# A new order for the start of a retention and feed-forward kernel: the heads' keys and states ahead of and between the first up units, and another hand-written order for block 1

## The chip, the cores and the metric

The kernel runs on one core of a Trainium2 chip. The metric is the device time of one execution in microseconds. The kernel before has a median of 298.65 us in three runs (297.25 to 298.95). A profiled execution of the same program gives the trace that all readings come from; its times count from the start of its span.

## The reference

Eight batches of eight heads, a sequence of 576, a head dimension of 64. Retention attention: scores of queries and keys, weighted by a decay that falls with the distance of the positions, times the values. The result is read as 4608 tokens of width 512 and goes through a feed-forward part with 2048 hidden units.

```python
scores = scale * np.matmul(q, k.transpose(0, 1, 3, 2))
gamma = 1.0 - 2.0 ** (-5.0 - np.arange(H, dtype=np.float32))
Dmat = np.where(rel >= 0, gamma[:, None, None] ** rel[None, :, :], 0.0)
ret = scores * Dmat[None, :, :, :]
return np.matmul(ret, v).astype(np.float32)
...
h = x @ w_in
relu6 = np.clip(h + 3.0, 0.0, 6.0)
g = h * relu6 / 6.0
return (g @ w_out).astype(np.float32)
```

## The kernel before, in words

The tokens are worked on in nine blocks of 512. Block 0 holds the "heads", the first 64 tokens of all eight batches; blocks 1 to 8 hold the other 512 tokens of one batch each, in four chunks of 128 (numbered 4 to 35). Each block goes through three stages.

*Retention.* Inside a chunk the scores are computed directly; what earlier tokens contribute comes through a state of 64x64 per head, which is multiplied by a decay from chunk to chunk. For the heads: `values_heads` (L449, result hpv), `scores_heads`, `inner_heads` (result hpo, copied into xT of block 0), `keys_heads` (L457: the keys turned by four groups of eight matmuls hpk, each followed by two scalings with a column of `dec` on ScalarE, L462), and `head_states` (L272: products pu, multiplied by the chunk's decay `gpow` into `zh`). For a chunk c, with the letter that stands for each step in the written order:
- c, `casts` (L182): key cast, query and value times decay, on ScalarE, GpSimd and VectorE. For the chunks in `Q_DVE` the second half of the query is done by VectorE (L192).
- t, `transposes` (L198): keys and queries turned by TensorE into ptk and ptq, copied to kT (ScalarE) and qT (VectorE) at L211.
- a, `scores` (L244) into pa; `masked` (L263, multiplications at L267); s, `states` (L291), products into the other half of pa (from chunk 8 on chunks go in pairs, and pu has banks of its own).
- u, `add` (L314): two additions on VectorE (L317, L320) and one decay multiplication on GpSimd (L321) carry the state z to the next chunk.
- z, `past` (L323): the state copied to fp16 by ScalarE (L327; L329 and L330 for a block's first chunk).
- x, `cross_over`: queries times the past state into po; i, `inner`: scores times values into the same po, then two casts into xT of the block (L373).

*Up product.* 16 units per block. A unit (`up_steps`, L495) is eight matmuls (a head's rows at a time, L153) into a bank ph, a Relu on ScalarE (L514, u) and a combined minimum and product on VectorE (L516) that gives g and frees the bank. `up_two` (L529) does two units for only one half of the block's tokens: L is the left half, R the right half, U a whole unit. The left half needs xT of the first two chunks only. H holds back the g instructions of half units, G gives them out.

*Down product.* For blocks 0 and 1 `down_plain` (L573): 64 steps of two matmuls, into four banks pd_0 to pd_3 of 16 steps each. pd_0 and pd_1 are filled in turn, four steps each, then pd_2 and pd_3; so pd_0 ends with step 28, pd_1 with 32, pd_2 with 60, pd_3 with 64, and each is copied out by ScalarE (L585) right behind its last step. D is a step of the older block, E one of the younger. From block 2 on `down_strassen` (L591) does seven products of halves, whose operands are sums of weights (`weight_sums`, L673) and of g; these sums are made on VectorE (L556) by `+`. The end of the last block has an order of its own (L637 to L651): the adds of c21 and c22 free the banks that the last product (3, by_e) takes.

The order is written by hand. `tc.manual_schedule` covers all five engines: each engine runs its instructions in the order in which the program issues them. `go` (L721) plays a string of letters with numbers; there is one for block 1's up product beside block 0's down product, and one for block 2's beside block 1's. After that tables (STEADY) serve every block. PSUM has six banks "pp" (ph, pa, pu, po, ptk, ptq, hpk, hpo) and two banks "st" (hpv, pd and the products of `down_strassen`); an instruction that takes a bank waits for the last reader of what was in it.

The transfers: GpSimd issues the input weights win (five DMAs, L687) and the output weights wout (four, L692) early, then the 16 small instructions `arg` (L123, L124) of `decays`, then mask and `gpow`. SyncE issues the loads of chunks fk, fq, fv (L174, L178); the first of them waits for the first piece of wout (`fetch(8, wout[0])`).

Of the kernel before, what the change touches and what calls it, by code (L numbers as in the profile page):

```python
# [12 lines left out]
FP32 = mybir.dt.float32  # L13
FP16 = mybir.dt.float16
# [7 lines left out]
def kernel(  # L22
# [64 lines left out]
    zh = [const.tile([P, NP, D], FP32, name=f"zh{b}") for b in range(B)]  # L87
# [32 lines left out]
    def decays():  # L120
        for h in range(H):
            lg = float(np.log(gamma[h]))
            nc.gpsimd.tensor_scalar(arg[:, :, h], fj[:, 0:4], lg, float(np.log(D ** -0.5)), ALU.mult, ALU.add)  # L123
            nc.gpsimd.tensor_scalar(arg[:, :, H + h], fj[:, 0:4], -lg, 0.0, ALU.mult, ALU.add)  # L124
        nc.scalar.activation(dec, arg, ACTF.Exp)
# [100 lines left out]
    Q_DVE, K_POOL, KT_DVE = (4, 6), (7, 8, 9, 10, 11, 13), (12, 13)  # L226
# [45 lines left out]
    def head_states(c):  # L272
        pu = [psum.tile([P, NP, D], FP32, tag="pp", name=f"pu{e}_{c}") for e in range(2)]
        todo = ([], [])
        for i in range(NP):
            for a in range(2):
                j, h2 = divmod(i + NP * a, 2)
                for e in range(2):
                    todo[e].append(mm(pu[e][rows(a), i], kn[rows(e), j, c, h2 * D:h2 * D + D],
                                      vh[rows(e), c, j, h2, :], start=True, stop=True))  # L280
        in_turn(todo)
        nc.vector.tensor_tensor(zh[c], pu[0], decay, ALU.mult)
        if c < 2:
            nc.vector.tensor_tensor(zh[c + NCB], pu[1], decay, ALU.mult)
        else:
            nc.scalar.copy(zh[c + NCB], pu[1])
            nc.gpsimd.tensor_tensor(zh[c + NCB], zh[c + NCB], decay, ALU.mult)
# [3 lines left out]
    def states(c0):  # L291
# [14 lines left out]
        if len(g) == 1:  # L306
            masked(c0)
# [6 lines left out]
    def add(c):  # L314
        kb, i0 = divmod(c, NCB)
        z = state_of(c)
        nc.vector.tensor_tensor(z[:, 1], sums[c][0], z[:, 0] if i0 else zh[kb - 1], ALU.add)  # L317
# [4 lines left out]

    def past(c):  # L323
        kb, i0 = divmod(c, NCB)
        z16 = work.tile([P, 2, NP, D], FP16, tag="z16", bufs=2, name=f"z16_{c}")
        if i0:
            nc.scalar.copy(z16, zs[c])  # L327
        else:
            nc.scalar.copy(z16[:, 0], zh[kb - 1])  # L329
            nc.scalar.copy(z16[:, 1], zs[c][:, 1])  # L330
        z16s[c] = z16
# [125 lines left out]
    def keys_heads(i):  # L457
# [449 lines left out]
```

## Time and profile before

| | |
|---|---|
| median of three runs | 298.65 us (297.25 to 298.95) |
| profiled execution | 297.9 us |
| its span in the trace | 296.2 us, 12622 instructions |
| granted TensorE clock | 1.0 |
| TensorE matmuls | 285.1 us busy, 5574 |
| VectorE | 216.0 us busy, 374 |
| ScalarE | 186.6 us busy, 330 |
| GpSimd | 135.7 us busy, 172 |
| DMA | 47.86 MB, mean 162 GB/s |

How to read the rows below. A timeline row is: start in us from the span's start, length in us, engine, line in the kernel, operation, result <- operands, partitions and elements, xcount (instructions of one kind that stand in a row), and in brackets how long the engine was idle before and what ended that. Matmul ends are modelled and the matmuls are pipelined, so the length of a group includes the time that its last result takes; the distance from one start to the next is the better measure. PE is TensorE, DVE VectorE, ACT ScalarE, POOL GpSimd, SPq the DMA issues of SyncE. The page's row of the chain gives the shares of the span by what held the work up that ended last.

### The profile page before, as it was taken

How to read it: one execution, taken by the hardware profiler on the slowest of the kernel's cores; microseconds unless marked ns; L12 is line 12 of the kernel's file. 1: busy time of each engine (PE TensorE's matmuls, PEld its weight loads, DVE VectorE, ACT ScalarE, POOL GpSimd, SP SyncE). 2: the span in 40 equal slices, each digit the busy share in tenths (PEclk: the TensorE clock that was granted, in tenths of full speed). 3: DMA queues.
4: the chain of work that ended last, by engine and by line, in shares of the span. 5: the costliest groups of instructions: out<-in, count | busy, mean ns of one | idle time of the engine just before them, and what ended most of it. 6: DMA issues, size and time to landing. Idle time of an engine off the chain costs nothing.

```text
span 296.2 us, 12622 instructions
## 1 busy us (share of the span) xinstructions
PE 285.1 (96%) x5574; PEld 221.2 (75%) x5574; DVE 216.0 (73%) x374; ACT 186.6 (63%) x330; POOL 135.7 (46%) x172
## 2 busy tenths in 40 slices
PE   4998999999999999999999999999999999999995
PEld 2775655878665669887877878878788978778894
DVE  8738768868875778598886887697868786647654
ACT  3838855676775778575776668567756674655420
POOL 8971046795834625239624762566255003100510
PEclk9999999999999999999999999999999999999999
DMA  7999999999999999988999999699915101200114
GB/s 165 147 174 213 224 217 233 241 232 222 170 151 243 180 211 159 243 217 182 248 226 205 203 223 152 162 199 229 130 46 100 73 6 52 92 2 2 73 73 142
DMA packets 119542, 47.86 MB, mean 162 GB/s; under 512 B 92352, under 2 KB 114880, under 8 KB 119488
## 3 DMA queue, kind: packets, MB, share of 16 engines
q1 hardware_dynamic: 114336, 41.56, 70.8%
q0 software_dynamic: 4720, 5.11, 10.7%
q8 instruction: 43, 0.70, 1.0%
q10 hardware_dynamic: 432, 0.39, 0.5%
q14 instruction: 11, 0.09, 0.2%
HBM read 36.70 MB, written 9.44 MB: 156 GB/s over the span
## 4 chain that ended last, share of the span: by engine, by line
PE 78%; DMA 6%; POOL 6%; DVE 5%; ACT 2%; issue 2%; POOLq 0%; ACTq 0%; DVEq 0%
PE ph L153 38%; PE pm L153 29%; PE pd L153 4%; DMA win<-in_moe_w_in_dram 3%; DMA fq<-in_q_dram 3%; PE po L232 3%; PE pu L232 2%; DVE g L516 2%; POOL hv L443 2%; PE pa L232 1%; POOL hk L403 1%; POOL q L192 1%; DVE g L543 1%; ACT u L514 1%; DVE a L267 1%
## 5 line engine op out<-in xcount | busy, mean ns | idle before, releaser
L153 PE MATMUL ph<-xT,win 128*64 128x512 f16 (+1 forms) x1248 | 145.7, 364 | 2.0 <-DMA win<-in_moe_w_in_dram 1.7
L516 DVE SCALAR_TENSOR_TENSOR g<-u,ph 128x512 f16<-128x512 f32 x132 | 89.7, 684 | 52.7 <-ACT u L514 52.0
L514 ACT ACTIVATE u<-ph,half 128x512 f32<-128x512 f32 x132 | 90.2, 690 | 41.7 <-PE ph L153 40.8
L153 PEld LDWEIGHTS <-win 128*64 128x64 f16 x1248 | 84.6, 136 | 28.6 <-DMA win<-in_moe_w_in_dram 2.3
L153 PEld LDWEIGHTS <-g 128*64 128x64 f16 x928 | 52.5, 110 | 14.7 <-issue 0.3
L153 PEld LDWEIGHTS <-s 128*64 128x64 f16 x896 | 50.8, 110 | 8.0 <-issue 0.2
L321 POOL TENSOR_TENSOR z<-z,gpow 128x256 f32<-128x256 f32 x24 | 16.1, 670 | 67.7 <-DVE z L320 52.5
L153 PE MATMUL pm<-ws,s 128*64 128x256 f16 x672 | 45.9, 273 | 0.0
L192 POOL TENSOR_TENSOR q<-fq,dec 128x512 f16<-128x512 f32 x30 | 35.6, 1204 | 17.3 <-DMA fq<-in_q_dram 17.3
L373 ACT CAST xT<-po 128x512 f16<-128x512 f32 (+1 forms) x36 | 21.8, 680 | 23.7 <-PE po L232 23.7
L620 POOL TENSOR_TENSOR u<-u,p 128x512 f32<-128x512 f32 x7 | 8.9, 1268 | 60.3 <-ACT u L660 54.0
L195 POOL TENSOR_TENSOR v<-fv,dec 128x512 f16<-128x512 f32 x32 | 36.0, 1125 | 0.0
L153 PE MATMUL pd<-wout,g 128*64 128x512 f16 x256 | 34.1, 381 | 0.0
L153 PE MATMUL pm<-wout,g 128*64 128x256 f16 x448 | 32.2, 273 | 0.0
L267 DVE TENSOR_TENSOR a<-pa,mask 128x512 f16<-128x512 f32 (+1 forms) x36 | 21.0, 625 | 4.9 <-PE pa L232 2.6
L556 DVE TENSOR_TENSOR s<-g 128x1024 f16<-128x1024 f16 x28 | 19.4, 695 | 0.2
L327 ACT CAST z<-z 128x512 f16<-128x512 f32 x24 | 15.0, 624 | 5.8 <-DVE z L317 5.7
L188 ACT CAST k<-fk 128x512 f16<-128x512 f32 x26 | 16.2, 622 | 1.0 <-DMA fk<-in_k_dram 1.0
L153 PE MATMUL pm<-ws,g 128*64 128x256 f16 x224 | 16.7, 274 | 0.0
L153 PE MATMUL pm<-wout,s 128*64 128x256 f16 x224 | 16.5, 273 | 0.1
L556 DVE TENSOR_TENSOR s<-g,s 128x1024 f16<-128x1024 f16 x14 | 13.0, 925 | 0.0
L543 DVE SCALAR_TENSOR_TENSOR g<-u,ph 128x512 f16<-128x512 f32 x12 | 8.0, 683 | 4.7 <-ACT u L542 4.6
(112 smaller groups left out, 288.1 us busy)
## 6 DMA issues: line engine op xcount, KB each, us to landing
fk<-in_k_dram SPq DMA_DIRECT2D x32, 256.0 KB, 4.8
fq<-in_q_dram SPq DMA_DIRECT2D x16, 512.0 KB, 5.9
fv<-in_v_dram SPq DMA_DIRECT2D x32, 256.0 KB, 5.6
out_dram<-o SPq DMA_DIRECT2D x14, 512.0 KB, 4.0
wout<-in_moe_w_out_dram POOLq DMA_DIRECT2D x4, 512.0 KB, 18.0
out_dram<-o SPq DMA_DIRECT2D x7, 256.0 KB, 4.2
win<-in_moe_w_in_dram POOLq DMA_DIRECT2D x3, 512.0 KB, 11.6
hq<-in_q_dram SPq DMA_DIRECT2D x6, 128.0 KB, 4.3
```

The source lines that it names most:

```text
L153: nc.tensor.matmul(out[r], lhs[:, r], rhs, skip_group_check=True, **flags)
L188: (nc.gpsimd.tensor_copy if c in K_POOL else nc.scalar.copy)(by_head(k16), in_rows(st[c]["fk"]))
L192: (nc.vector if e and c in Q_DVE else nc.gpsimd).tensor_tensor(by_head(q16[:, e]), in_rows(st[c]["fq"][:, :, e, :]), in_rows(dd[:, 2 + e, ...
L195: nc.gpsimd.tensor_tensor(v16, st[c]["fv"], dd[:, 1, H:2 * H, :], ALU.mult)
L232: return lambda: nc.tensor.matmul(*args, skip_group_check=True, **flags)
L267: nc.vector.tensor_tensor(a16[:, a, 0:n].rearrange("p x i q -> p (x i) q"), pa[a].rearrange("p x i q -> p (x i) q"), m, ALU.mult)
L321: nc.gpsimd.tensor_tensor(new, new, decay, ALU.mult)
L327: nc.scalar.copy(z16, zs[c])
L373: nc.scalar.copy(xt[:, s], po[s].rearrange("p x n (e r) -> p x n e r", e=2))
L514: nc.scalar.activation(uu[:, 0:n], ph[:, 0:n], ACTF.Relu, bias=half, scale=1.0 / 6.0)
L516: nc.vector.scalar_tensor_tensor(out=g[:, hf, ths, jr, :], in0=by_half(uu), scalar=1.0, in1=by_half(ph), op0=ALU.min, op1=ALU.mult)
L556: nc.vector.tensor_tensor(*pend.popleft())
```

## The change

- `decays` is split. The eight `arg` columns for keys now stand on GpSimd ahead of the wout issues, the eight for queries and the mask behind them; `gpow` ahead of the last wout issue. The exponents are two instructions in place of one: for keys behind inner_heads(0)'s copy on ScalarE, for queries behind unit 12 of block 0.
- `keys_heads` moves from between block 0's down steps to the place ahead of the first up units; keys 0 and 1 take "st" banks and are scaled by ScalarE, keys 2 and 3 take "pp" banks and are scaled by VectorE.
- `head_states` now does two chunks at a time and stands behind the first four up units. Its decay multiplications are four steps of 128x512 (`heads_decayed`): two on VectorE, two as a ScalarE copy with a GpSimd multiplication, behind units 3, 4, 9 and 10. `zh` is one tile.
- Q_DVE loses chunk 6; the second half of its query goes to GpSimd.
- The masks of single chunks get a letter of their own, m, and stand behind the adds u. The two copies of `past` for a block's first chunk are split (y for the heads' state). p and r turn keys and queries apart. The weight sums are queued as 3, 1, 2, 4 per half.
- The two order strings are new. The first begins with 24 plain down steps; blocks of eight down steps stand ahead of r4, z4 and z5; the half units L come right behind i5 and i6, and R4 right behind t8; the last unit of block 1 stands at the end of the first string.
- In the last block's end, the first half of c22 is added before c21, the second behind it.

```diff
...
@@ -117,12 +117,17 @@
         for h in (2 * i, 2 * i + 1):
             nc.scalar.activation(hmask[:, h, :], dist, ACTF.Exp, bias=scale, scale=float(np.log(gamma[h])))
 
-    def decays():
+    def decays(of):
         for h in range(H):
             lg = float(np.log(gamma[h]))
-            nc.gpsimd.tensor_scalar(arg[:, :, h], fj[:, 0:4], lg, float(np.log(D ** -0.5)), ALU.mult, ALU.add)
-            nc.gpsimd.tensor_scalar(arg[:, :, H + h], fj[:, 0:4], -lg, 0.0, ALU.mult, ALU.add)
-        nc.scalar.activation(dec, arg, ACTF.Exp)
+            if of == "q":
+                nc.gpsimd.tensor_scalar(arg[:, :, h], fj[:, 0:4], lg, float(np.log(D ** -0.5)), ALU.mult, ALU.add)
+            else:
+                nc.gpsimd.tensor_scalar(arg[:, :, H + h], fj[:, 0:4], -lg, 0.0, ALU.mult, ALU.add)
+
+    def exponents(of):
+        part = slice(0, H) if of == "q" else slice(H, 2 * H)
+        nc.scalar.activation(dec[:, :, part], arg[:, :, part], ACTF.Exp)
 
     def decays_of_chunk():
         for h in range(H):
@@ -223,7 +228,7 @@
 
 
     PAIRS = 8
-    Q_DVE, K_POOL, KT_DVE = (4, 6), (7, 8, 9, 10, 11, 13), (12, 13)
+    Q_DVE, K_POOL, KT_DVE = (4,), (7, 8, 9, 10, 11, 13), (12, 13)
     group = lambda c: [c] if c < PAIRS else [c, c + 1]
     rows = lambda x: slice(SUB * x, SUB * x + SUB)
     gs = {}
@@ -269,22 +274,27 @@
 
     decay = gpow.unsqueeze(2).to_broadcast([P, NP, D])
 
-    def head_states(c):
-        pu = [psum.tile([P, NP, D], FP32, tag="pp", name=f"pu{e}_{c}") for e in range(2)]
+    def head_states(c0, tag):
+        pu = [psum.tile([P, 2, NP, D], FP32, tag=tag, name=f"pu{e}_{c0}", **(dict(bufs=2) if tag == "st" else {}))
+              for e in range(2)]
         todo = ([], [])
-        for i in range(NP):
-            for a in range(2):
-                j, h2 = divmod(i + NP * a, 2)
-                for e in range(2):
-                    todo[e].append(mm(pu[e][rows(a), i], kn[rows(e), j, c, h2 * D:h2 * D + D],
-                                      vh[rows(e), c, j, h2, :], start=True, stop=True))
+        for c in (c0, c0 + 1):
+            for i in range(NP):
+                for a in range(2):
+                    j, h2 = divmod(i + NP * a, 2)
+                    for e in range(2):
+                        todo[e].append(mm(pu[e][rows(a), c - c0, i], kn[rows(e), j, c, h2 * D:h2 * D + D],
+                                          vh[rows(e), c, j, h2, :], start=True, stop=True))
         in_turn(todo)
-        nc.vector.tensor_tensor(zh[c], pu[0], decay, ALU.mult)
-        if c < 2:
-            nc.vector.tensor_tensor(zh[c + NCB], pu[1], decay, ALU.mult)
+        return pu
+
+    def heads_decayed(c0, e, pu):
+        z, by = zh[:, c0 + NCB * e:c0 + NCB * e + 2], gpow.unsqueeze(1).unsqueeze(3).to_broadcast([P, 2, NP, D])
+        if e:
+            nc.scalar.copy(z, pu[e])
+            nc.gpsimd.tensor_tensor(z, z, by, ALU.mult)
         else:
-            nc.scalar.copy(zh[c + NCB], pu[1])
-            nc.gpsimd.tensor_tensor(zh[c + NCB], zh[c + NCB], decay, ALU.mult)
+            nc.vector.tensor_tensor(z, pu[e], by, ALU.mult)
 
     zs, z16s, sums = {}, {}, {}
 
@@ -303,8 +313,6 @@
                         todo[s].append(mm(pu[s][rows(a), x, i], k16[rows(s), i, a, :], v16[rows(s), i + NP * a, :],
                                           start=True, stop=True))
         in_turn(todo)
-        if len(g) == 1:
-            masked(c0)
 
     def state_of(c):
         if c not in zs:
@@ -314,21 +322,24 @@
     def add(c):
         kb, i0 = divmod(c, NCB)
         z = state_of(c)
-        nc.vector.tensor_tensor(z[:, 1], sums[c][0], z[:, 0] if i0 else zh[kb - 1], ALU.add)
+        nc.vector.tensor_tensor(z[:, 1], sums[c][0], z[:, 0] if i0 else zh[:, kb - 1], ALU.add)
         if i0 < NCB - 1:
             new = state_of(c + 1)[:, 0]
             nc.vector.tensor_tensor(new, sums[c][1], z[:, 1], ALU.add)
             nc.gpsimd.tensor_tensor(new, new, decay, ALU.mult)
 
+    def past_of_heads(c):
+        z16s[c] = work.tile([P, 2, NP, D], FP16, tag="z16", bufs=2, name=f"z16_{c}")
+        nc.scalar.copy(z16s[c][:, 0], zh[:, c // NCB - 1])
+
     def past(c):
-        kb, i0 = divmod(c, NCB)
-        z16 = work.tile([P, 2, NP, D], FP16, tag="z16", bufs=2, name=f"z16_{c}")
-        if i0:
-            nc.scalar.copy(z16, zs[c])
+        if c % NCB:
+            z16s[c] = work.tile([P, 2, NP, D], FP16, tag="z16", bufs=2, name=f"z16_{c}")
+            nc.scalar.copy(z16s[c], zs[c])
         else:
-            nc.scalar.copy(z16[:, 0], zh[kb - 1])
-            nc.scalar.copy(z16[:, 1], zs[c][:, 1])
-        z16s[c] = z16
+            if c not in z16s:
+                past_of_heads(c)
+            nc.scalar.copy(z16s[c][:, 1], zs[c][:, 1])
 
     xts = {}
 
@@ -454,12 +465,16 @@
                 product(pv[:, c], pick[:, j, c, :], hd[i]["v"][:, :, j, :], start=(j == 0), stop=(j == NJ - 1))
         copy(vh[:, :, i], pv)
 
-    def keys_heads(i):
-        pk = psum.tile([P, NCB, 2, D], FP32, tag="pp", name=f"hpk{i}")
+    def keys_heads(i, tag, on_dve):
+        pk = psum.tile([P, NCB, 2, D], FP32, tag=tag, name=f"hpk{i}", **(dict(bufs=2) if tag == "st" else {}))
         for c in range(NCB):
             product(pk[:, c].rearrange("p a d -> p (a d)"), hd[i]["kT"][:, c, :], ident16, start=True, stop=True)
         for a in range(2):
-            nc.scalar.mul(kn[:, i, :, a * D:a * D + D], pk[:, :, a, :], dec[:, 0, H + 2 * i + a:H + 2 * i + a + 1])
+            to, by = kn[:, i, :, a * D:a * D + D], dec[:, 0, H + 2 * i + a:H + 2 * i + a + 1]
+            if on_dve:
+                nc.vector.tensor_scalar(to, pk[:, :, a, :], by, None, ALU.mult)
+            else:
+                nc.scalar.mul(to, pk[:, :, a, :], by)
 
     def scores_heads(i):
         kT, qT = hd[i]["kT"], hd[i]["qT"]
@@ -637,11 +652,11 @@
             yield from one(7, by_c, True)
             for m in range(2):
                 add(dve, u3[:, m], by_c[m], p1[:, m])
+            yield from one(5, by_e)
+            add(dve, c22[:, 0], by_e[0], u3[:, 0])
             add(dve, c21, bd, u3)
             store(kb, 1, o2, cols=lo)
-            yield from one(5, by_e)
-            for m in range(2):
-                add(dve, c22[:, m], by_e[m], u3[:, m])
+            add(dve, c22[:, 1], by_e[1], u3[:, 1])
             store(kb, 1, o2, cols=hi)
             for m in range(2):
                 yield from one(3, by_e, True, (m,))
@@ -715,8 +730,10 @@
             if what == "+":
                 side_sums(c)
             elif c < NCH:
-                {"c": cast, "t": lambda c: transposes(c, True, "kq" if c < PE_T else "k" if c < PE_K else ""), "a": scores, "s": states, "u": add, "z": past,
-                 "x": cross_over, "i": inner, "k": keys_heads, "h": head_states, "o": lambda _: store(*kept.popleft())}[what](c)
+                {"c": cast, "t": lambda c: transposes(c, True, "kq" if c < PE_T else "k" if c < PE_K else ""),
+                 "p": lambda c: transposes(c, True, "k"), "r": lambda c: transposes(c, True, "q"),
+                 "a": scores, "s": states, "m": masked, "u": add, "y": past_of_heads, "z": past,
+                 "x": cross_over, "i": inner, "o": lambda _: store(*kept.popleft())}[what](c)
 
     def go(plan, kb=None, down=None, ahead=None):
 
@@ -781,7 +798,12 @@
         win_piece(0, 2)
         for n in (1, 2, 3):
             win_piece(n)
-        wout = [wout_piece(pc) for pc in (0, 2, 1, 3)]
+        decays("k")
+        wout = [wout_piece(pc) for pc in (0, 2, 1)]
+        decays_of_chunk()
+        wout.append(wout_piece(3))
+        decays("q")
+        mask_of_chunk()
         distances()
         idle_products(5)
         mask_of_heads(0)
@@ -812,10 +834,15 @@
         scores_heads(3)
         values_heads(1, on_act)
         inner_heads(0, on_act)
+        exponents("k")
         values_heads(2, on_dve)
         inner_heads(1, on_dve)
         values_heads(3, on_act)
         inner_heads(2, on_dve)
+        keys_heads(0, "st", False)
+        keys_heads(2, "pp", True)
+        keys_heads(3, "pp", True)
+        keys_heads(1, "st", False)
         first = [up_steps(0, u) for u in range(4)]
         for dmc in range(3):
             for unit in first:
@@ -825,23 +852,29 @@
         for unit in first:
             for _ in unit:
                 pass
-        decays()
-        mask_of_chunk()
-        decays_of_chunk()
+        heads = [head_states(0, "pp"), head_states(2, "st")]
         fetch(8, wout[0])
+        heads_decayed(0, 0, heads[0])
         for u in range(4, NFC):
             up_unit(0, u)
-        weight_sums(3)
-        weight_sums(1, 2, 4)
+            if u == 4:
+                heads_decayed(0, 1, heads[0])
+            elif u == 9:
+                heads_decayed(2, 0, heads[1])
+            elif u == 10:
+                heads_decayed(2, 1, heads[1])
+            elif u == 12:
+                exponents("q")
+        weight_sums(3, 1, 2, 4)
         down, ahead = down_plain(0), down_plain(1)
-        go("k0 D4 k1 D4 +1 k2 D4 +1 k3 D5 h0 h1 D4 c4 h2 h3 D8 t4 c5 +1 D7 a4 s4 u4 +1 D3 t5 D5 z4 x4 a5 s5 i4 u5 z5 +1 c6 +1 D7 "
-           "x5 D2 i5 D4 t6 c7 L2 H0 L2 a6 s6 u6 G0 L2 t7 z6 L2 H0 L2 x6 a7 s7 i6 u7 G0 z7 D6 L2 c8 x7 D1 i7 t8 E4 "
-           "c9 R4 t9 c10 R2 c11 E2 a8 s8 u8 E2 R2 z8 u9 t10 E4 z9 t11 c12 R2 E2 R2 c13 E4 a10 x8 s10 i8 "
-           "u10 U1 z10 t12 u11 U1 t13 z11 U1 U1 c14 E4 a12 x10 s12 i10",
+        go("D8 +2 D8 +2 D8 +1 c4 D8 p4 D8 r4 c5 y4 +1 D4 t5 a4 s4 u4 m4 D8 z4 x4 c6 a5 s5 i4 u5 m5 D8 z5 x5 D2 i5 +1 L2 p6 r6 c7 "
+           "L2 H0 L2 a6 s6 u6 m6 G0 L2 t7 z6 H0 L2 x6 a7 s7 i6 u7 m7 G0 z7 L2 c8 x7 D2 i7 +1 t8 "
+           "c9 R4 t9 c10 R2 c11 E4 a8 s8 u8 E2 R2 z8 u9 t10 E4 z9 t11 c12 R2 E2 R2 c13 E6 a10 x8 s10 i8 "
+           "u10 U1 z10 t12 u11 U1 t13 z11 U1 c14 E6 a12 x10 s12 i10 u12 c15 U1",
            1, down, ahead)
         down = ahead
-        go("u12 c15 D7 z12 +1 U1 D3 u13 U1 D3 z13 +1 U1 D2 c16 U1 D3 U1 D3 U1 D2 U1 D1 U1 D5 a14 x12 s14 i12 u14 U1 c17 z14 +1 U1 D1 u15 U1 D1 z15 o1 "
-           "U1 +1 U1 D1 U1 D1 c18 U1 U1 D5 a16 x14 s16 i14 u16 +1 D4",
+        go("D3 z12 +1 U1 D4 u13 U1 D3 z13 +1 U1 D2 c16 U1 D3 U1 D3 U1 D3 U1 D1 U1 D5 a14 x12 s14 i12 u14 U1 c17 z14 +1 U1 D1 u15 U1 z15 o1 "
+           "U1 +1 U1 D1 U1 c18 U1 U1 D7 a16 x14 s16 i14 u16 +1 D4",
            2, down)
         for kb in range(2, NB):
             for _ in down:
```

## The prediction on record

> **What bounds the kernel now.** I read the page first: the span, the busy shares, the chain by engine.
>
> ```profile
> span 296.2 us, 12622 instructions
> ...
> PE 285.1 (96%) x5574; PEld 221.2 (75%) x5574; DVE 216.0 (73%) x374; ACT 186.6 (63%) x330; POOL 135.7 (46%) x172
> ...
> PE 78%; DMA 6%; POOL 6%; DVE 5%; ACT 2%; issue 2%; POOLq 0%; ACTq 0%; DVEq 0%
> ```
>
> TensorE is the bound: 285.1 of 296.2 us, and no other engine is above 73%. The diff leaves the matrix products as they are in number and size (moved, not removed), so the time can change only where TensorE stands still: fewer or more stalls, and what is computed inside stalls that remain. I therefore read the timeline of PE gap by gap, first its front.
>
> ```profile
> 18.50 1.95 PE L153 MATMUL ph<-xT,win 128*64 128x512 f16 x16 [0.72 <-DMA win<-in_moe_w_in_dram]
> ...
> 23.42 1.95 PE L153 MATMUL ph<-xT,win 128*64 128x512 f16 x16 [0.98 <-DMA win<-in_moe_w_in_dram]
> ...
> 33.83 0.39 PE L153 MATMUL hpk<-ident,hkT 128*64 128x128 f16 x8
> 34.05 1.03 PE L153 MATMUL pd<-wout,g 128*64 128x512 f16 x8
> ...
> 38.49 0.45 PE L232 MATMUL pu<-ws,ws 64*64 64x64 f16 x32
> ...
> 39.85 0.56 PE L232 MATMUL pu<-ws,ws 64*64 64x64 f16 x32
> ```
>
> Before the first up units and again before unit 4, PE waits for the input weights: at 18.50 after 0.72 us, at 23.42 after 0.98. The keys of the heads (hpk) and their states (pu) are paid later, between down steps: one hpk group takes 34.05-33.83 = 0.22, four take 0.88; two pu groups take 0.45+0.56 = 1.0. Together 1.9.
>
> **A. The front.** The change puts hpk ahead of the first up unit and pu between units 3 and 4, into the two stalls. How much fits depends on what they wait for.
>
> ```profile
> 15.81 1.65 POOL L692 DMA_DIRECT2D wout<-in_moe_w_out_dram  x3
> ...
> 19.35 0.19 POOL L123 TENSOR_SCALAR arg<-fj 128x4 f32<-128x4 f32 x1
> ...
> 22.25 0.20 POOL L124 TENSOR_SCALAR arg<-fj 128x4 f32<-128x4 f32 x1
> ```
>
> ```profile
> 17.60 0.58 ACT L455 CAST ws<-hpv 128x512 f16<-128x512 f32 x1 [1.16 <-PE hpv L153]
> ...
> 24.12 0.27 ACT L125 ACTIVATE dec<-arg 128x64 f32<-128x64 f32 x1
> ```
>
> ```profile
> 22.55 2.48 DVE L516 SCALAR_TENSOR_TENSOR g<-u,ph 128x512 f16<-128x512 f32 x4 [4.03 <-ACT u L514]
> ```
>
> The 16 arg rows stand from 19.35 to 22.45, 0.2 each; eight of them, now ahead of the wout issues at 15.81, take 1.6 to 1.8 and end near 17.6. The exponents are behind them on ACT and, in program order, ahead of its copy of hpv3 (now 17.60): 0.27 ends at about 17.9, the copy of 0.58 at 18.5. The last hpk group takes the bank which that copy frees: 0.22, so PE turns to the up product at about 18.8 in place of 18.5. The first four units end 0.1 later (their last pieces wait for the hpo3 copy, also 0.3 later), near 22.5; the states then take about 0.85, to 23.4. Unit 4 needs a bank from the first g, which with the same shift ends at 22.55+0.69+0.3 = 23.5; so unit 4 starts near 23.6, not 23.42. Of the 1.9 all but 0.2 is therefore hidden: **-1.7 to -1.8**, I take -1.8 with the switch between tile sizes that goes. If the weights were to land sooner, the cover would be gone and all 1.9 paid here; nothing shows that.
>
> **B. Stalls of before that go.**
>
> ```profile
> 42.09 0.39 PE L153 MATMUL ptk<-ident,k 128*64 128x128 f16 x8
> 42.65 0.64 PE L153 MATMUL ptq<-ident,q 128*64 128x128 f16 x16 [0.17 <-POOL q L192]
> ...
> 47.46 0.26 PE L232 MATMUL po<-qT,z 64*64 64x64 f16 x8 [0.21 <-ACT z L330]
> ...
> 51.77 0.39 PE L153 MATMUL ptk<-ident,k 128*64 128x128 f16 x8
> 52.23 0.64 PE L153 MATMUL ptq<-ident,q 128*64 128x128 f16 x16
> ```
>
> A ptk group takes 0.22 when nothing is awaited, here it is 42.65-42.09 = 0.56 and 52.23-51.77 = 0.46 to the next: 0.34 and 0.24 are lost. x4 loses 0.21 and its switch, some 0.38 (the z copy came late: masks stood ahead of the z adds on VectorE). The new order puts eight down steps between p4 and r4, adds ahead of masks, and eight steps ahead of z4: **-0.95**.
>
> **C. New stalls in block 1.** Each is a step of PE that needs a copy made from PE's own result, with less work put between them than the copies take. The rows for the length of such a chain:
>
> ```profile
> 43.77 1.03 PE L153 MATMUL pd<-wout,g 128*64 128x512 f16 x8
> ...
> 50.88 1.05 PE L153 MATMUL pd<-wout,g 128*64 128x512 f16 x8
> ...
> 54.92 1.09 PE L153 MATMUL ph<-xT,win 128*64 128x256 f16 x16
> 55.85 0.39 PE L153 MATMUL ptk<-ident,k 128*64 128x128 f16 x8
> 56.07 1.92 PE L153 MATMUL ph<-xT,win 128*64 128x256 f16 x32
> ```
>
> ```profile
> 43.98 0.58 ACT L585 COPY o<-pd 128x512 f32<-128x512 f32 x1 [0.30 <-PE pd L153]
> ...
> 51.00 0.76 ACT L373 CAST xT<-po 128x256 f16<-128x256 f32 x2 [0.70 <-PE po L232]
> ...
> 57.16 0.63 ACT L327 CAST z<-z 128x512 f16<-128x512 f32 x1
> ```
>
> - x5: the last of the eight steps before it ends pd_2, whose copy stands ahead of the copy of z_5 on ACT. The copy begins 0.21 after PE has left the bank (43.98 against 43.77), then 0.58 less 0.1 overlap, then 0.63: **1.3**.
> - The first L2 after i5 needs xT from that very i5. The casts start 0.12 after PE has gone on (51.00 against 50.88) and take 0.76: 0.88, less 0.05 for the switch: **0.83**. Before, four down steps and t6 lay between (50.88 to 51.77 is 0.89 for the four alone).
> - The L2 after i6 needs xT from i6 at its third product: 0.88 less two products of 0.05: **0.78**. Before, six down steps lay there.
> - R4 after t8 needs xT from i7: 0.88 less t8 (0.22) and the switch: **0.6**. Before, four steps lay there.
> - x6: behind the fourth L2 come u_10, the copy of kT_7 and z_6 on ACT. In before the same three end at 57.16+0.63 = 57.79, 1.94 after their L2 ended (55.85), and t7 and two L2 (0.22+1.84) covered them. Now t7 and one L2 (0.22+0.93) do: **0.8**.
> - a6: g of the first half unit stands ahead of both qT_6 casts on VectorE; a unit (0.69 ACT, 0.69 DVE) and two casts (1.29 below) make 2.1 after r6 against two L2 of 0.9: **0.35**. a4, by the same casts behind the work for c5, **0.15**.
>
> ```profile
> 43.11 1.29 DVE L211 CAST qT<-ptq 128x512 f16<-128x512 f32 x2 [0.75 <-PE ptq L153]
> ```
>
> Sum of C: 1.3+0.83+0.78+0.6+0.8+0.35+0.15 = **+4.8**. The bounds are 1.3 (all but x5 covered by something I overlooked) and 5.6 (each chain 0.1 slower).
>
> **D. Pairs, and the end of block 1.**
>
> ```profile
> 81.16 0.22 PE L232 MATMUL pu<-v,k 64*64 64x64 f16 x2 [0.17 <-DVE g L516]
> 81.76 0.44 PE L232 MATMUL pu<-v,k 64*64 64x64 f16 x30 [0.38 <-DVE g L516]
> ```
>
> ```profile
> 82.73 1.34 ACT L373 CAST xT<-po 128x512 f16<-128x512 f32 x2 [1.26 <-PE po L232]
> 83.91 0.63 ACT L188 CAST k<-fk 128x512 f16<-128x512 f32 x1
> ...
> 85.51 0.70 ACT L514 ACTIVATE u<-ph,half 128x512 f32<-128x512 f32 x1
> ```
>
> ```profile
> 86.24 0.69 DVE L516 SCALAR_TENSOR_TENSOR g<-u,ph 128x512 f16<-128x512 f32 x1 [1.88 <-ACT u L514]
> ```
>
> The state products wait there for a bank that g frees: 0.55, and smaller waits like it come to about 1.3. Six down steps in place of four ahead of a10 and a12 take most of that away. Against it, the last unit of block 1 (U15) now follows i10: ACT has two xT casts (1.34), a key cast (0.63) and u (0.70) to do, then DVE g (0.69), 3.3 with the overlaps, before the fourth down step of the next plan can read that g; PE has two units and three steps to do meanwhile, 2.4: 0.9. s12 takes a bank behind it, no row of its own, between 0 and the 0.55 above; I take 0.5, its nearest row, and 0.2 for small ones. Net **+0.3** (between -1.1 and +0.8).
>
> **E. The end.**
>
> ```profile
> 290.85 1.94 PE L153 MATMUL pm<-wout,s 128*64 128x256 f16 x32
> ```
>
> ```profile
> 292.01 0.43 DVE L620 TENSOR_TENSOR o<-pm,u 128x256 f32<-128x256 f32 x1 [0.77 <-PE pm L153]
> ```
>
> The last block adds half of c22 before c21 and half behind it. The second half frees its bank about one add of 0.7 later than now; the second half of the last product (16 of the 32 products) waits for it about 0.2, and the two last adds and the store follow: **+0.2** (0 to 0.4).
>
> **Removed instructions elsewhere** (six 128x256 multiplications on DVE become two of 128x512, half of q_6 goes to POOL) are at nothing: both engines have idle time there, and POOL's q_6 is wanted only some 3 us after it can be ready. If that cover fails, 1.1 at most.
>
> **Sum.** -1.8 -0.95 +4.8 +0.3 +0.2 = +2.5, between -2.2 and +4.0. The profiled execution took 297.9 us (span 296.2 and 1.7 around it), the median of the runs is 298.65, 0.75 above it. On the median this gives 301.1; I say **301.0**.
>
> **The rivals.**
> 1. *Faster.* An engine that waits lets the others catch up, so after the 1.3 of x5 later copies may be ready in time. Then A, B and the waits of D remain: -1.8-0.95+1.3-0.9+0.2 = -2.2, 296.5. Against it: the chains of C begin at PE's own results (i5, i6, i7, the fourth L2), and a lead of the other engines doesn't shorten those. Chance 0.17.
> 2. *No change.* a4, a6, x6 and s12 are covered after all, the chains with nothing between (x5, two L2, R4) remain: -1.8-0.95+3.5-0.2+0.2 = +0.75, 299.4. For it: four of my waits are differences of two long sums. Chance 0.25.
> 3. *Slower still, through the loads.* The eight arg instructions hold the wout issues back by 1.7. SP's first loads go out when wout's first piece has landed:
>
> ```profile
> 30.95 0.42 SPq L174 DMA_DIRECT2D fk<-in_k_dram  x1
> ```
>
> ```profile
> 41.15 1.45 POOL L192 TENSOR_TENSOR q<-fq,dec 128x512 f16<-128x512 f32 x1 [17.29 <-DMA fq<-in_q_dram]
> ```
>
> ```profile
> wout<-in_moe_w_out_dram POOLq DMA_DIRECT2D x4, 512.0 KB, 18.0
> ```
>
> If wout lands 1.7 later, q_4 is ready at 44.3 in place of 42.6, while r4 comes near 42.9: about 1.3 more, 302.4. It decides from a delay of about 0.4 on. Against it: 18.0 us from issue to landing for 512 KB means that wout waits behind others, so a later issue should wait less. Chance 0.06. The Trainium skill ("DMA: Bandwidth & Descriptors", section "Issuing engines are not separate DMA queues") says that DMAs of all issuing engines run on the same 16 engines and interleave; by that rule the bytes ahead decide and not the moment of issue, the 18.0 agrees, and the sum would stay.
>
> **How the numbers follow.** My forecast, +2.4 give or take 1.2, has 0.52; no change 0.25; faster 0.17; slower still 0.06. The likeliest case's own range is 299.9 to 302.2. Reaching to the cases beside it until 2 in 10 are out gives 297.2 to 302.8. A measurement of this kernel can tell about 0.5% (1.5 us) from no change: faster 0.17, same 0.25, slower 0.58 from the cases above.
>
> **What would show it.** In the changed profile: the hpk rows before the first ph row, unit 4 at about 23.6, the first pd row near 34.0 with no pu behind it (A); no wait at x4 (B); po at x5 behind the z copy, ph rows with waits on ACT xT after i5, i6, i7 (C); pd behind a DVE g at the start of block 2 (D). I am wrong if PE's waits between 45 and 70 us come to less than 2 us, or if fq lands later than 41.

## The result, and the profile after

The changed kernel takes 301.32 us (median of four runs, 300.63 to 302.28) against 298.36 of before; the ratio is 1.0106, with a 95% interval of 1.0063 to 1.0149. In a second set of six runs beside later experiments the ratio was 1.0136 (1.0090 to 1.0182). It is slower by 3 to 4 us; the forecast was 301.0. The profiled execution took 300.63 us. (A ratio here is that of all runs of a kernel to those of before beside them on the same chip; it can differ from the quotient of the two medians by some tenths of a percent.)

The page of the changed kernel, the same three rows as above:

```profile
span 298.9 us, 12627 instructions
...
PE 285.5 (95%) x5574; PEld 227.8 (76%) x5574; DVE 214.4 (72%) x373; ACT 186.0 (62%) x327; POOL 136.1 (46%) x173
...
PE 85%; DVE 7%; ACT 6%; issue 2%; POOL 0%; ACTq 0%; DVEq 0%; POOLq 0%
```

PE is as busy as before (285.5 against 285.1), and the span is 2.7 longer: nearly all of it is time in which PE waits. In the chain that ended last, the DMA's 6% and GpSimd's 6% are gone, and ACT has 6% in place of 2%: from 18 us on PE no longer waits for transfers, it waits for copies of its own results. The view of waits, PE alone, from 30 to 295 us (columns: who waits, for what, us in all, times, longest), first of before and then of the changed kernel:

```profile
PE pu L232 <- DVE g L516: 0.7, 3, 0.4
PE ph L153 <- issue: 0.3, 1, 0.3
PE po L232 <- ACT z L330: 0.2, 1, 0.2
PE ptq L153 <- POOL q L192: 0.2, 1, 0.2
```

```profile
PE po L237 <- ACT z L338: 1.9, 2, 1.2
PE ph L158 <- ACT xT L384: 1.7, 3, 0.8
PE pd L158 <- DVE g L531: 0.7, 1, 0.7
PE pa L237 <- DVE qT L216: 0.3, 1, 0.3
PE pu L237 <- DVE g L531: 0.3, 1, 0.3
```

1.4 us of waits became 4.9: z at x5 and x6, xT at three half units, g of the last unit, qT at a6. ("issue" in before's list means that no semaphore released PE there; the last section comes back to it.) The front first, by the timeline of PE in the changed kernel:

```profile
18.20 1.06 PE L158 MATMUL hpk<-ident,hkT 128*64 128x128 f16 x32
...
22.90 0.74 PE L237 MATMUL pu<-ws,ws 64*64 64x64 f16 x64
23.82 0.44 PE L158 MATMUL ph<-xT,win 128*64 128x512 f16 x2 [0.19 <-DVE g L531]
...
34.18 2.17 PE L158 MATMUL pd<-wout,g 128*64 128x512 f16 x18
```

All keys and states are done when unit 4 starts at 23.82 (23.42 before), and the first down step starts at 34.18, 0.35 later than the first hpk of before, with 1.9 us of work done ahead. Its q_4 was there in time (GpSimd's part ended near 42.3, its products began at 43.04). Then block 1:

```profile
50.87 0.26 PE L237 MATMUL po<-qT,z 64*64 64x64 f16 x8 [1.20 <-ACT z L338]
...
52.83 1.09 PE L158 MATMUL ph<-xT,win 128*64 128x256 f16 x16 [0.84 <-ACT xT L384]
...
56.68 0.32 PE L237 MATMUL pa<-qT,kT 64*64 64x64 f16 x16 [0.34 <-DVE qT L216]
...
59.93 0.26 PE L237 MATMUL po<-qT,z 64*64 64x64 f16 x8 [0.68 <-ACT z L338]
...
61.48 0.77 PE L158 MATMUL ph<-xT,win 128*64 128x256 f16 x10 [0.59 <-ACT xT L384]
...
64.54 1.97 PE L158 MATMUL ph<-xT,win 128*64 128x256 f16 x32 [0.23 <-ACT xT L384]
...
87.30 1.05 PE L158 MATMUL pd<-wout,g 128*64 128x512 f16 x8 [0.70 <-DVE g L531]
```

In order these are x5, the L2 after i5, a6, x6, the L2 after i6, R4, and the down step that needs g of U15. What holds x5 is read on ACT, one row above the other:

```profile
49.71 0.59 ACT L600 COPY o<-pd 128x512 f32<-128x512 f32 x1 [1.03 <-PE pd L158]
50.19 0.62 ACT L338 CAST z<-z 128x512 f16<-128x512 f32 x1
```

ACT was idle for 1.03 us, then copied pd_2, and only then z_5, though z was there from 48.2 on (its last add on VectorE starts at 47.74 and takes 0.42): the order of the program alone kept it. What the prediction named as signs of being wrong did not show: the waits between 45 and 70 us come to 3.9 us, not less than 2, and fq landed at 40.66, not later than 41.

### The profile page after: what moved, and what is told of

Read it like the earlier page. It is cut to its first block, busy times and chain, and to the rows that moved or that the text cites. A ratio compares the mean times of both kernels' runs of the same rounds, so it can differ in the third digit from the quotient of the medians.

```text
span 298.9 us, 12627 instructions
## 1 busy us (share of the span) xinstructions
PE 285.5 (95%) x5574; PEld 227.8 (76%) x5574; DVE 214.4 (72%) x373; ACT 186.0 (62%) x327; POOL 136.1 (46%) x173
## 4 chain that ended last, share of the span: by engine, by line
PE 85%; DVE 7%; ACT 6%; issue 2%; POOL 0%; ACTq 0%; DVEq 0%; POOLq 0%
PE ph L158 37%; PE pm L158 29%; PE pd L158 8%; PE po L237 3%; DVE g L531 2%; PE pa L237 2%; PE pu L237 2%; ACT u L529 1%; ACT xT L384 1%; PE hpv L158 1%; DVE early L110 1%; DVE qT L216 1%; ACT u L557 1%; ACT z L338 1%; PE idle L158 1%
## 5 line engine op out<-in xcount | busy, mean ns | idle before, releaser
L158 PEld LDWEIGHTS <-win 128*64 128x64 f16 x1248 | 88.0, 136 | 25.1 <-issue 2.3
L158 PEld LDWEIGHTS <-g 128*64 128x64 f16 x928 | 55.8, 110 | 14.7 <-DVE g L531 1.2
L329 POOL TENSOR_TENSOR z<-z,gpow 128x256 f32<-128x256 f32 x24 | 15.0, 627 | 70.5 <-DVE z L328 56.3
L197 POOL TENSOR_TENSOR q<-fq,dec 128x512 f16<-128x512 f32 x31 | 36.2, 1188 | 9.7 <-DMA fq<-in_q_dram 9.7
L158 PE MATMUL pd<-wout,g 128*64 128x512 f16 x256 | 32.5, 380 | 0.7 <-DVE g L531 0.7
L237 PE MATMUL po<-qT,z 64*64 64x64 f16 x512 | 10.8, 196 | 2.0 <-ACT z L338 1.9
```

Source lines behind the costliest of these rows:

```text
L158: nc.tensor.matmul(out[r], lhs[:, r], rhs, skip_group_check=True, **flags)
L197: (nc.vector if e and c in Q_DVE else nc.gpsimd).tensor_tensor(by_head(q16[:, e]), in_rows(st[c]["fq"][:, :, e, :]), in_rows(dd[:, 2 + e, ...
L237: return lambda: nc.tensor.matmul(*args, skip_group_check=True, **flags)
L329: nc.gpsimd.tensor_tensor(new, new, decay, ALU.mult)
```

## The experiments

The theory after the result: the change is two things. The front does 1.9 us of work in a stall, but block 1 can't begin sooner than the load of q_4 allows, so the lead is not yet time; the new order fills the lead with down steps, and those steps are then missing as cover between PE's results and their use. Rivals: the terms simply add (the front keeps its 1.6 by itself, the 1.9 less the 0.35 by which the down steps start later); the waits of block 1 come from the lead, not from the order; waits that are removed come back at the next place.

**The front alone** (the old order, without its k and h steps; q_6 and the end of the last block are those of before, too):

```diff
-go("k0 D4 k1 D4 +1 k2 D4 +1 k3 D5 h0 h1 D4 c4 h2 h3 D8 t4 ...
+go("D4 D4 +1 D4 +1 D5 D4 c4 D8 t4 ...
```

> The front of the change alone (keys of the heads ahead of the first up units, states behind the first four, keys' decays ahead of wout), with the old order of block 1, from which only the k and h steps are taken out. Theory 'the terms add': the profile after shows the first down step at 34.18 with the 1.9 us of keys and states already done, so the time falls by 1.6, to 0.994 to 0.995 of before. Rival 'the load of q_4 holds block 1': in after fq landed at 40.66, and POOL's q_4 takes 1.45 more, 42.1 to 42.6; the old order would reach ptq4 at about 40.6 now, so PE waits there some 1.5 to 2.0 us, and the time is that of before within 0.4 us (ratio 0.999 to 1.001).

Measured: 298.49 us, ratio 1.0017 (0.9990 to 1.0045). The rival held: no gain. Its timeline of PE shows where it went (the profiled execution was the slowest of the twelve, 301.41 us):

```profile
40.10 0.41 PE L158 MATMUL ptk<-ident,k 128*64 128x128 f16 x8
42.81 0.64 PE L158 MATMUL ptq<-ident,q 128*64 128x128 f16 x16 [2.30 <-POOL q L197]
```

PE reaches ptq 2 us sooner than before and waits for q_4 until the time at which it had it before (42.65 there).

**The front alone, loads sooner**:

```diff
-fetch(8, wout[0])
+fetch(8, last_win)
```

> As the front alone, and the first loads of block 1 wait for the last piece of win in place of the first piece of wout (27.04 against 29.86 in the profile after), so they go out 2.8 us sooner. If the load of q_4 holds block 1 in the front alone, fq lands near 38 now, the wait at ptq4 goes, and the time is 1.2 to 1.8 us below that of the front alone, unless wout comes late in its turn (its last piece is read at step 25, near 39.5). If the terms add, nothing waits for fq there, and it is the same as the front alone within 0.4 us.

Measured: 299.54 us, ratio 1.0022 (0.9991 to 1.0053). The load's issue moved by 4.0 us, its landing by less than one; SP's first issue and GpSimd's q_4 in the front alone, and then with loads sooner:

```profile
30.99 0.42 SPq L179 DMA_DIRECT2D fk<-in_k_dram  x1
...
41.30 1.46 POOL L197 TENSOR_TENSOR q<-fq,dec 128x512 f16<-128x512 f32 x1 [9.37 <-ACT kT L216]
```

```profile
26.98 0.42 SPq L179 DMA_DIRECT2D fk<-in_k_dram  x1
...
40.42 1.46 POOL L197 TENSOR_TENSOR q<-fq,dec 128x512 f16<-128x512 f32 x1 [7.88 <-DMA fq<-in_q_dram]
```

(In the first, fq landed at 41.14; the view names an ACT copy that ended about then.) The wait at ptq fell from 2.30 to 0.91 in this profile, 0.5 of it because PE came there later (ptk at 40.58 in place of 40.10), but the expected 1.2 to 1.8 us did not come. Even the 0.9 by which q_4 began sooner doesn't stand out: in the eight profiles with this front, all of wout and the loads behind its first piece (SP's first load at 29.07 to 30.99), q_4 began at 39.70 to 41.30, and in the second kernel with loads sooner, further down, at 41.15 after a first load at 27.52. Here issuing the load 2 to 4 us sooner brought nothing that can be told from that.

**The front alone, with half of wout not loaded**:

```diff
-wout = [wout_piece(pc) for pc in (0, 2, 1)]
+wout = [wout_piece(pc) for pc in (0, 2)]
...
+for pc in (1, 3):
+    nc.gpsimd.memset(wout16[:, JQ * pc:JQ * pc + JQ, :], 0.0)
```

> The front alone with two of the four pieces of wout (1 MB) not loaded but set to zero by GpSimd, so the results are of a wout that is half zero; every other instruction is as in the front alone. It tells whether bytes hold q_4. Theory: until 41 us the transfers move some 210 to 230 GB/s, so 1 MB less lets fq land 4 to 4.5 us sooner, near 36.5; the wait of 2.30 us at ptq4 goes, and the time is 2.0 to 2.4 below the front alone, 0.992 to 0.994 of before: what the front saves is then kept. Rival: fq's landing follows SP's issue time (30.99) by a fixed 9 to 10 us, and stays at 41; the time stays that of the front alone.

Measured: 297.09 us, ratio 0.9948 (0.9918 to 0.9977), 0.7% or 2.1 us below the front alone. q_4 starts five us sooner than in the front alone, and its products follow the keys' with no wait:

```profile
36.24 1.14 POOL L197 TENSOR_TENSOR q<-fq,dec 128x512 f16<-128x512 f32 x1 [4.41 <-DMA fq<-in_q_dram]
```

```profile
39.86 0.39 PE L158 MATMUL ptk<-ident,k 128*64 128x128 f16 x7
40.09 0.22 PE L158 MATMUL ptq<-ident,q 128*64 128x128 f16 x1
```

SP's first load, which waits for the first piece of wout, went out 1.15 sooner here as well. That this isn't the cause is seen on the changed kernel, which issued at the same time and had all of wout under way; first that kernel, then the one with half of wout:

```profile
29.88 0.41 SPq L179 DMA_DIRECT2D fk<-in_k_dram  x1
...
40.82 1.46 POOL L197 TENSOR_TENSOR q<-fq,dec 128x512 f16<-128x512 f32 x1 [8.42 <-DMA fq<-in_q_dram]
```

```profile
29.84 0.42 SPq L179 DMA_DIRECT2D fk<-in_k_dram  x1
```

From an issue at the same time, q_4 begins 4.6 us sooner. So what else is being transferred holds q_4, not the time of its issue (bytes and packets were taken away together, so this doesn't part the two). With q_4 there in time this kernel is some 1.6 us (0.52%) below before. Not all of that need be the front's: 0.34 of it can be before's own wait between ptk4 and ptq4, and no run has the old front with half of wout.

**The new order alone** (old front; the change's order, with the k and h steps among its first down steps, and its q_6 and end of the last block), twice, the second time with the sums later (the cut shows the second):

```diff
-go("D8 +2 D8 +2 D8 +1 c4 D8 p4 D8 r4 c5 y4 +1 ...
+go("k0 D4 k1 D4 +1 k2 D4 k3 D4 +1 h0 h1 D8 c4 h2 h3 D8 +2 p4 D8 +1 r4 c5 y4 +1 ...
```

> The new order of block 1 with the old front: keys and states of the heads stand between the first down steps again, everything else of block 1, block 2 and the end is as in the changed kernel. Theory of the prediction: the waits at x5, the L2 after i5, a6, x6, the L2 after i6, R4 and g15 come from the short distance between PE's own result and its use, so they all stay (4.5 to 4.9 us before chunk 8 and 0.9 at g15), and the time is 1.6 to 2.0 above that of the changed kernel: 1.015 to 1.018 of before. Rival: the waits come because the front lets PE run ahead of loads and of the other engines; with 2 us less lead they shrink by 2 us in all, and the time is that of the changed kernel or below (1.004 to 1.010).

> The new order of block 1 with the old front, as in the run of the order alone, but with the sums of weights queued behind the heads' states (in that run they overwrote the keys from which the states are made, so its states were of other numbers, with the same instructions). Theory: the waits of the new order stay, 1.015 to 1.018 of before. Rival: 1.004 to 1.010.

Measured: 303.29 us, ratio 1.0168 (1.0134 to 1.0202), and 303.62 us, ratio 1.0174 (1.0145 to 1.0203). The waits of PE in the second:

```profile
PE po L232 <- ACT z L328: 1.9, 2, 1.2
PE ph L153 <- ACT xT L374: 1.7, 3, 0.8
PE pd L153 <- DVE g L517: 0.7, 1, 0.7
```

These three are those of the changed kernel to a tenth; the wait for qT at a6 is longer, 0.6 against 0.3. The lead is not their cause; the order costs 5 us with the old front, and the front takes 1 to 2 of them back.

**z_5 one step sooner** in the changed kernel:

```diff
-... i4 u5 m5 D8 z5 x5 D2 i5 ...
+... i4 u5 m5 D7 z5 D1 x5 D2 i5 ...
```

> The changed kernel with one letter moved: z5 ahead of the last of the eight down steps, so its copy stands ahead of the copy of pd_2 on ACT. Theory: the wait at x5 (1.20 us in the profile after, ended by the copy of z) goes to 0.1 or so, and the time falls by 1.0 to 1.2 (0.996 of the changed kernel). Rival 'given back': the copy of pd_2 then stands between i5's casts and PE, the next wait (the L2 after i5, 0.84) grows by as much, and the time stays within 0.4 us.

Measured: 300.47 us, ratio to before 1.0071 (1.0040 to 1.0101), where the changed kernel has 1.0106 and 1.0136. The wait at x5 is gone and isn't given back at the L2 after i5:

```profile
49.70 0.26 PE L237 MATMUL po<-qT,z 64*64 64x64 f16 x8
...
51.66 1.09 PE L158 MATMUL ph<-xT,win 128*64 128x256 f16 x16 [0.85 <-ACT xT L384]
```

From t5 to R4 (44.50 to 63.38) it takes 1.31 us less than the changed kernel (44.35 to 64.54). By the times alone the intervals overlap; the profile decides.

**Covers put back** in the changed kernel:

```diff
-... m4 D8 z4 ... m5 D8 z5 x5 D2 i5 +1 L2 ... G0 z7 L2 c8 ...
+... m4 D4 z4 ... m5 D6 z5 x5 D2 i5 +1 D4 L2 ... G0 z7 D2 L2 c8 ...
```

> The changed kernel with six of its down steps moved: four from ahead of z4 and two from ahead of z5; four now stand ahead of the first L2 behind i5, two ahead of the L2 behind i6. The end of pd_2 thereby falls behind x5. Theory of the prediction: x5 falls from 1.2 to 0.1 or 0.2, the first L2 from 0.84 to 0.1, the L2 behind i6 from 0.8 to 0.4, x4 gains 0.15; the time falls by 1.8 to 2.3 (1.003 to 1.005 of before). Rival 'given back': the steps are missed where they were, x4 and x5 wait by as much for z, and the time stays within 0.5 us of the changed kernel.

Measured: 299.03 us, ratio 1.0011 (0.9989 to 1.0033). From t5 to R4 it takes 2.21 us less (44.55 to 62.53); the two waits of xT that are left come to 0.4:

```profile
PE po L237 <- ACT z L338: 0.7, 1, 0.7
PE ph L158 <- ACT xT L384: 0.4, 2, 0.2
```

z at x5 and xT at the first L2 are covered, and nothing came in their place but 0.3 inside i4, which now waits for the masks. Moving six steps that were already there takes most of the loss away.

**U15 sooner**:

```diff
-... z11 U1 c14 E6 a12 x10 s12 i10 u12 c15 U1
+... z11 U1 U1 c14 E6 a12 x10 s12 i10 u12 c15
```

> The changed kernel with the last unit of block 1 (U15) put back ahead of c14, as in before. Theory: g15 is made long before the fourth down step of the next string; the wait there (0.70 us on DVE g in the profile after, 0.92 by the distance of starts) goes and the time falls by 0.7 to 0.9 (0.9975 of the changed kernel). Rival: the wait only moves to s12, which then takes its bank behind that g: no change within 0.3.

Measured: 302.39 us, ratio 1.0144 (1.0118 to 1.0171), no better than the changed kernel. The theory missed, and of the rival only the time came true: the wait moved, but to another place. The wait for g is gone, but U15 had covered i10's way to xT; the first unit of block 2 now waits for that:

```profile
84.26 0.84 PE L158 MATMUL pd<-wout,g 128*64 128x512 f16 x6
85.80 1.08 PE L158 MATMUL ph<-xT,win 128*64 128x512 f16 x8 [0.70 <-ACT xT L384]
```

In before seven down steps stood there, here three. From a10 to the second unit of block 2 it takes 12.16 us (75.45 to 87.61), in the changed kernel 12.14 (76.05 to 88.19). The unit and the steps have to move together.

**A mixed order**: the changed kernel's front and 40 steps ahead of r4, then the order of before with 24 steps in place of 35.

```diff
+go("D8 +2 D8 +2 D8 +1 c4 D8 p4 D8 r4 c5 y4 +1 D4 t5 D1 a4 s4 u4 m4 D4 z4 x4 c6 a5 s5 i4 u5 m5 D5 z5 x5 D2 i5 +1 D1 t6 c7 "
+   "L2 H0 L2 a6 s6 u6 m6 G0 L2 t7 z6 L2 H0 L2 x6 a7 s7 i6 u7 m7 G0 z7 D5 L2 c8 x7 D2 i7 +1 t8 E4 c9 R4 ...
```

> The changed kernel's front and its 40 down steps ahead of r4 (so that PE has work until q_4 is there), and behind it the order of before, with its 35 down steps cut to 24: t6 in one piece ahead of the first L2, two L2 ahead of x6, five steps ahead of the L2 behind i6, four E steps ahead of R4, the last units as before. Theory 'the waits are missing cover': of the 4.9 us before chunk 8 in the changed kernel about 0.6 stay (0.15 at x4, 0.2 at x5, 0.2 at the first L2), g15's 0.9 goes, and the time is 3.5 to 4.3 below that of the changed kernel, 0.993 to 0.996 of before. Rival 'the cover cannot be had': 24 steps are too few and the waits turn up at other places; the time is that of before or above (1.000 to 1.005).

Measured: 297.54 us, ratio 0.9969 (0.9938 to 1.0000), the lowest ratio of all that use the whole wout: clearly below the changed kernel, and below before by 0.3%, at the edge of what can be told. The theory's 0.993 to 0.996 was just missed, the rival's 1.000 to 1.005 lies above the measured ratio. Its waits of PE from 30 to 295 us:

```profile
PE pd L158 <- issue: 0.9, 1, 0.9
PE ptq L158 <- POOL q L197: 0.6, 1, 0.6
PE pa L237 <- DMA qT<-q: 0.5, 1, 0.5
PE ph L158 <- issue: 0.3, 1, 0.3
```

Of the changed kernel's waits none is in the list. By the distances from start to start something is left: at x5 the five down steps before it take 1.51 us (46.95 to 48.46), where eight without a wait take 1.85, so some 0.35 of the 1.27 stay; and i4 now waits 0.3 for the masks.

**The second half of q_6 back on VectorE** in the mixed order, and then **loads sooner** besides, with three steps moved behind r4:

```diff
-Q_DVE, K_POOL, KT_DVE = (4,), ...
+Q_DVE, K_POOL, KT_DVE = (4, 6), ...
```

> The mixed order with the second half of q_6 given back to VectorE, as in before. In the profile of the mixed order PE waits 0.59 at the second half of ptq6 for GpSimd's q, whose two halves take 2.43 behind a transfer that lands at 48.5, while VectorE is idle from 49.0 to 50.4. Theory: the wait goes, 0.5 to 0.6 less than the mixed order: 0.994 to 0.996 of before. Rival: VectorE's part waits for the same transfer and delays z or qT: no change.

> As the last one, with the first loads behind the last piece of win (as in the run of the front with loads sooner, where fq landed 0.4 to 0.9 sooner), so three of the 40 steps ahead of r4 can go behind it: one more ahead of z4, two more ahead of z5. In the mixed order PE waits 0.33 inside i4 (masks) and 0.44 at x5 (z). Theory: these fall by 0.5 in sum and ptq4 doesn't wait: 0.5 below the last one, 0.992 to 0.995 of before. Rival: ptq4 waits by what the steps gave: no change.

Measured: 298.26 us, ratio 0.9995 (0.9967 to 1.0024), and 297.52 us, ratio 0.9982 (0.9954 to 1.0011). Neither beats the mixed order. The first one's profile has no wait at ptq6 and a span of 294.5, but its twelve runs spread from 295.89 to 299.72. The second one's profile (of an execution of 299.85 us, next to its slowest) shows how the rival comes about, first VectorE, then PE:

```profile
48.98 0.69 DVE L197 TENSOR_TENSOR q<-fq,dec 128x512 f16<-128x512 f32 x1 [2.00 <-DMA fq<-in_q_dram]
49.59 0.42 DVE L325 TENSOR_TENSOR z<-pa,z 128x256 f32<-128x256 f32 x1
```

```profile
50.71 0.26 PE L237 MATMUL po<-qT,z 64*64 64x64 f16 x8 [1.40 <-ACT z L338]
```

VectorE stands 2.00 us at q_6, whose load isn't there, and the add of z_5 is queued behind it. In the first one's profile the load was there, and VectorE did q_6 at 47.03 without a wait. So that part of the change (q_6 to GpSimd) belongs with the sooner c6: it keeps a transfer that may be late from holding z. How often it is late, and whether that spreads the runs of the first, was not shown.

**The changed kernel again**:

> The changed kernel again, beside these on one chip: 1.008 to 1.011 of before by its first four runs.

Measured: 301.98 us, ratio 1.0136 (1.0090 to 1.0182). That is above the expected 1.008 to 1.011; one of the six runs took 305.34 us. Its profile has the same five waits (1.9, 1.7, 0.7, 0.3, 0.3), and 1.4 of "issue" besides.

## Why the prediction was right, point by point

- **The sum.** By the two profiles, stage by stage: the down steps start 0.35 later with 1.9 of work done ahead, -1.55 (A, -1.8 forecast). From there to R4 it takes 30.36 us; before took 29.41, or 26.64 without that work and without four E steps (0.87) that stood ahead of R4: +3.72 (B and C, +3.85 forecast; one by one, below, they come to 3.9). From R4 to the second unit of block 2 it takes 23.65 against 22.45, with three more steps (0.65) in it: +0.55 (D, +0.3 forecast). The rest comes to nothing (E, +0.2 forecast). Together +2.7, as the spans say. That 301.0 was so close is in part luck: A and D came out 0.25 dearer each, the others cheaper, and the second set gave 301.98. (The prediction's terms add to +2.55, which it takes as 2.5 and then as 2.4; its lower end, by the bounds given with the terms, is -2.55 in place of -2.2. Neither matters to the forecast.)
- **A, the front (-1.8).** The work fits the stalls as forecast; unit 4 at 23.82 against 23.6, the down steps at 34.18 against 34.0, the difference being that all of the heads' part ran some 0.6 late in this execution. That differs from execution to execution (23.35 and 33.71 in the front alone; 33.58 to 34.41 for the down steps in the eleven profiles with this front). But the prediction booked -1.8 as time. The front alone shows that it is none by itself: q_4's load takes it back. It counts only because the new order has 40 down steps ahead of r4, and these 11 more steps are the same that C misses. A and the covers of C are one account; the sum was right because both sides were in it.
- **B (-0.95).** Gone, as forecast: no wait at x4, t4 and t6 in the changed kernel's list.
- **C (+4.8).** By the distances from start to start, with the switches taken off, x5 1.27 (1.3 forecast), the L2 after i5 0.89 (0.83), a6 0.46 (0.35), x6 0.75 (0.8), the L2 after i6 0.85 (0.78), R4 0.34 (0.6), a4 0.29 (0.15): 4.85. R4 was priced too high: t8 turns keys and queries, three groups of 0.22, and I took the 0.22 of the keys alone. With all three it would have been 0.17; the other half came from what the price left out, the copy of pd_3, which stands ahead of the casts on ACT, so that they start 0.28 after PE went on (at 63.45) and not 0.12:

```profile
63.25 0.59 ACT L600 COPY o<-pd 128x512 f32<-128x512 f32 x1
63.73 0.76 ACT L384 CAST xT<-po 128x256 f16<-128x256 f32 x2
```

That the cause is missing cover is shown by four runs: z_5 sooner takes away x5's wait, the covers put back take 2.2, the order alone keeps them all with the old front, the mixed order has nearly none of them with the new front.

- **D (+0.3).** The wait for g15 came as priced (0.92 by distance, 0.9 forecast), and s12's 0.5 did not come; some of before's waits in the pairs stayed instead (0.29 at a bank that g frees). In sum D was 0.25 too low. Its cure failed, see U15 sooner.
- **E (+0.2).** From the start of the last product to the end of the span it is 298.9-293.46 = 5.44 us; before 296.2-290.85 = 5.35. So 0.1.
- **The rivals.** *Faster* fell: only if the chains shortened with the lead, and the order alone shows that they don't depend on it. *Slower through the loads* fell: wout was issued 1.4 later (17.17 against 15.81), and SP's first load, which waits for its landing, went out at 29.88, sooner than the 30.95 of before. The Trainium skill's rule ("DMA: Bandwidth & Descriptors", section "Issuing engines are not separate DMA queues") is that all DMAs run on the same engines and interleave. Three runs here agree with it: issue 1.4 later and no loss, issue 4.0 sooner and no gain that can be told, 1 MB less and five us gained. That what is under way decides, and not the moment of issue, is what these runs show; the page doesn't say it.

## What to carry to other kernels

Work put into a stall is time only if what comes next isn't held by something else; look for the transfer behind the next wait before booking a gain. A filler instruction has two uses, bridging a late transfer and covering the way from a result to its use, and it can be spent once: count what stands between each product of TensorE and the instruction that needs its copy, in both orders. Ahead of a short cover, the order of copies on ScalarE can be worth as much as the cover itself: one letter moved was worth 1.3 us here, six steps moved 2.2.

## What the runs showed of the hardware

PE stood in several profiles at places where no semaphore released it (the view says "issue"), for 0.2 to 1.5 us at a time, with other amounts in each kernel and even in two executions of the same one: 0 in the first profile of the changed kernel, 1.4 in the second, 2.4 in the run with loads sooner in the mixed order:

```profile
PE pd L158 <- issue: 2.4, 2, 1.5
```

They stood at the same product in several kernels (the pm products at 128 to 130 us in three of them). The traces show what most likely holds it. From 25 us on there are 25 such stretches in the profiles, in twelve of the fourteen; if one counts PE's products and weight loads from the start, every one of them stands 193 to 197 behind a multiple of 256. The page has a queue "instruction" with 43 transfers of 16 KB each (0.70 MB), and one of them had landed 1.2 to 1.6 us before the end of each stretch. Where it had landed earlier than that, there is no stretch. So PE waited there, in all likelihood, for the next piece of its own program; no run here was made to prove it.

Such a stretch can move a run by as much as most edits here (the twelve runs of the mixed order lie between 296.00 and 299.42), so effects below 1 us are read from the distances in the profiles. Without them the spans fit together better: the changed kernel's two profiles have 298.9 and 299.0 us, before has 295.9, the mixed order 294.4. By these single profiles the mixed order is 1.5 below before, where the runs show 0.3%.
